# A register as scale of the exponentials, and ScalarE instead of VectorE as reader of the first feed-forward layer's sums

## The chip, the cores and the metric

The kernel runs on one core of one Trainium2 chip. A core has four engines that compute: TensorE (PE in the profile) multiplies matrices into PSUM, VectorE (DVE), ScalarE (ACT) and GpSimd (POOL) do the elementwise work; SyncE (SP) issues the transfers. Each engine works through a queue of its own in order, and engines wait for each other on semaphores. The metric is the device time of one execution in microseconds (us), as the median of several runs. A profile, taken in a run of its own, shows when each instruction ran.

## The reference

One transformer block in which attention and a feed-forward network work in parallel on the same normalized input. All is float32, with 2048 rows of 512, 32 heads of 16, and 1792 hidden units.

```python
xn = _layernorm(x)
qkv = (xn @ wqkv) ...                       # 32 heads of 16
scores = einsum("bhqd,bhkd->bhqk", q, k) * 16 ** -0.5
p = softmax(scores); o = einsum("bhqk,bhkd->bhqd", p, v)
A = o.reshape(B, S, D) @ wo
h = gelu(xn @ w1 + b1)                      # tanh form
B = h @ w2 + b2
out = x + A + B
```

## The kernel before

**Numbers.** Float32 operands are divided by powers of two and split into a high and a low float16 part; a product is three float16 products (`PAIRS`). The factors come back later as scales: `sexp` (line 95) has, for each of four sets of eight heads, the factor of the scores times 16 ** -0.5, the same number in all 128 partitions; `fac1` has the factors of the first layer's weights, `gs` those of the others.

**The loop.** Attention is cut into 32 tiles: eight groups of four heads by four blocks of 512 queries. A tile has 16 units, one for each block of 128 keys, so there are 512 units (`NU`, line 387). `unit` (line 626) writes out one unit in two halves. In each half, TensorE computes two heads' scores in a first orientation (`s_half`, line 238, into a bank called pS), and VectorE takes their maximum (line 250). It also computes, for a unit that lies 19 (`LEAD`) back, two heads' scores in the transposed orientation with the maximum already subtracted (`e_half`, line 284, into pT), and ScalarE takes their exponential (line 295) into a buffer pe. Then it multiplies the exponentials of a still earlier unit with the values (`v_half`, line 298, into pV), and beside that, on the other 64 rows of the array, it does a few products of the dense work (`dense`, line 568, into pD). So in each unit VectorE has four reductions, ScalarE four exponentials, and TensorE's order of work is fixed by the order in which the program is written.

**Banks.** PSUM has eight banks: three for pS, three for pT, one for pD and one for pV at the start (`free_banks`, line 102). A dense group takes a bank when it begins (`dbank`, line 398) and gives it to the pT banks when it ends, so that the next group takes its bank from these: pD and pT share four banks, of which pD holds one. `tiled` and `product` (lines 195 and 167) issue all these products, so most of TensorE's rows carry line 169.

**The dense work.** Three generators feed the groups (`Group`, line 404): `rest` (the projections to queries and keys, whose sums ScalarE reads at line 495), `mlp` (line 995) and `tail` (the output projection, read at line 1100 while attention runs and at line 1093 after its scores are done). `mlp` runs four times over 512 rows: 14 groups of the first layer, 12 products for each side, at a pace of 4 or 3 products a half unit (`FAST`, `SLOW`), then four groups of the second layer with 42 products a side. When a first-layer group is over, `hidden` (line 1033) reads its sums out of PSUM, multiplies by the factor, adds the bias and writes hh (line 1036, VectorE). One unit later `gelu` (line 1001) begins: three steps on GpSimd, a tanh on ScalarE (line 1005), four more on GpSimd. When a second-layer group is over, ScalarE reads its sums (line 1059, yt). At the end of each tile ScalarE reads pV (line 321, osb).

**Bookkeeping.** `later` and `pooled` place work by slots, one slot a unit. `given` (line 159) adds an estimated time to `backlog`, which each half unit lowers by 1300 ns (line 660); no other line reads it.

Of the kernel before, what the change touches and what calls it, by code (L numbers as in the profile page):

```python
# [10 lines left out]
I32 = mybir.dt.int32  # L11
AF = mybir.ActivationFunctionType
ALU = mybir.AluOpType
# [14 lines left out]
NQB = S // QB  # L28
# [19 lines left out]
def layer_kernel(ctx: ExitStack, tc: tile.TileContext, x, wqkv, wo, w1, b1, w2, b2, out):  # L48
    nc = tc.nc
# [45 lines left out]
    sexp = const.tile([P, 4], F32, name="sexp")  # L95
# [11 lines left out]
    def banks(tag):  # L107
        k = free_banks[tag].pop(0)
        free_banks[tag].append(k)
        return bank_tile(k, tag)  # L110
# [48 lines left out]
    def given(engine, ns):  # L159
        backlog[engine] += ns  # L160
# [26 lines left out]
    def enter():  # L187

        if left:
            goal[0] = f"turn{counted[0]}"  # L190
            for p in left:
                tc.add_to_no_dep_group(goal[0], p.ins)
            left.clear()

    def tiled(user, dst, lhs, rhs, start, stop):

        for j in range(0, P, 32):
            product(user, dst[j:j + 32], lhs[:, j:j + 32], rhs, start=start, stop=stop)


    mt_of, ptiles, pv_of, stores = {}, {}, {}, {}
    queue, slot = [], [0]

# [22 lines left out]
    def tick():  # L226
        run_due()
        run_steps()
        slot[0] += 1
# [54 lines left out]
    def e_half(u, n):  # L284

        p, a = divmod(n, 2)
        t, kt = divmod(u, 16)
        g, qb = divmod(t, NQB)
        st = banks("T")
        r = slice(64 * a, 64 * a + 64)  # L290
        k0 = (kt % 4) * P
        tiled(None, st, kst[g % 2][p][kt // 4][r, k0:k0 + P], qst[g % 2][p][qb][r, :], True, True)
        pe = work.tile([P, QB], F32, name="pe", bufs=12)
        ptiles[u, n] = pe
        nc.scalar.activation(pe, st, AF.Exp, scale=sexp[:, g // 2:g // 2 + 1])  # L295
        given("act", 580)

    def v_half(u, a):

# [87 lines left out]
    NU = NG * NQB * 16  # L387
# [171 lines left out]
    def burst(gen, n):  # L559

        while n > 0 and (f := group(gen)) is not None:
            if not f.usable():
                break
            f.product(2)
            n -= 1
            ended()
# [59 lines left out]
    def unit(gen):  # L626


        u = pos[0]
        e = u - LEAD  # L630
        if u == LEAD and cur[0] is not None:
            burst(gen, cur[0].left())
        pos[0] += 1
        for a in range(2):
            for b in range(2 * a, 2 * a + 2):
                if u < NU:
                    s_half(u, b)
                elif u > NU:
                    spare(gen, b % 2)
                if 0 <= e < NU:  # L640
                    e_half(e, b ^ 1)
            if u < LEAD:
                burst(gen, LFILL[u - 16] // 2)
            if e >= 0:
                enter()

                w, r = (e - 2, 1) if a == 0 else (e - 1, 0)
                live = 0 <= w < NU
                new = r == 0 and w % 16 == 0
                if live and not new:  # L650
                    v_half(w, r)
                dense(gen, 1 - r)
                if live and new:
                    v_half(w, r)

                for user, goes_on in (("V", live and not (r == 1 and w % 16 == 15)),
                                      ("D", cur[0] is not None and not cur[0].over())):
                    leave(user, goes_on)
                for k in backlog:
                    backlog[k] = max(0, backlog[k] - HALF)  # L660
                if live and r == 1:
                    v_end(w)
                ended()

            if a == 0 and u % 16 == 0 and u // 16 - 1 in stores:
                stores.pop(u // 16 - 1)()
        if u < NU:
            s_end(u)
        tick()
# [325 lines left out]
    def mlp():  # L995
        m2 = st2p
        w2_s = m2.tile([P, 2, NF, D], F16, name="w2_s")
        b2_b = m2.tile([P, D], F32, name="b2_b")
        done = set()

        def gelu(hh, g, b, f):
            t1 = m2.tile([P, QB], F32, name="t1", bufs=2)

            def tanh():
                nc.scalar.activation(t1, t1, AF.Tanh, scale=GELU_C * GELU_A)
                given("act", 600)
                later(1, rest, True)

            def rest():
                pooled((690, lambda: nc.gpsimd.tensor_scalar(t1, t1, 1.0, gs[:, 1:2], op0=ALU.add, op1=ALU.mult)),  # L1010
                       (1280, lambda: nc.gpsimd.tensor_tensor(t1, t1, hh, op=ALU.mult)),  # L1011
                       (620, lambda: nc.gpsimd.tensor_scalar(g[:, 0, f, :], t1, 1.0, 0.0, op0=ALU.mult, op1=ALU.add)),
                       (1160, lambda: nc.gpsimd.tensor_tensor(g[:, 1, f, :], t1, g[:, 0, f, :], op=ALU.subtract)),  # L1013
                       (0, lambda: done.add((b, f))))

            pooled((1040, lambda: nc.gpsimd.tensor_tensor(t1, hh, hh, op=ALU.mult)),  # L1016
                   (620, lambda: nc.gpsimd.tensor_scalar(t1, t1, 1.0, 1.0 / GELU_A, op0=ALU.mult, op1=ALU.add)),
                   (1280, lambda: nc.gpsimd.tensor_tensor(t1, t1, hh, op=ALU.mult)),  # L1018
                   (0, lambda: later(2, tanh, True)))

        for b in range(NQB):
            xb = xbs[b]
            g = m2.tile([P, 2, NF, QB], F16, name="g", bufs=1)
            for f in range(NF):
                later(1, lambda n=b * NF + f + 2: fetch_w1(n))
                wc = wcs[b * NF + f]
                if b == 0 and f >= 3:
                    for k in range(f - 3, NF if f == NF - 1 else f - 2):
                        later(2 * (k - f + 3), lambda k=k: nc.sync.dma_start(w2_s[:, :, k], w2_d[:, :, k]))
                if b == 0 and f == 3:  # L1030
                    nc.sync.dma_start(b2_b, b2[None, :].to_broadcast([P, D]))

                def hidden(hp, g=g, b=b, f=f):
                    hh = m2.tile([P, QB], F32, name="hh", bufs=3)
                    scale, bias = fac1[0][:, f // 2:f // 2 + 1], b1_s[:, f:f + 1]
                    nc.vector.tensor_scalar(hh, hp, scale, bias, op0=ALU.mult, op1=ALU.add)  # L1036
                    given("dve", 700)
                    later(1, lambda: gelu(hh, g, b, f), True)

                yield Group([lambda c=c, i=i, j=j, wc=wc, xb=xb: (wc[:, i, c, :], xb[:, j, c, :])  # L1040
                             for c in range(NC) for i, j in PAIRS], dbank, hidden, pace=FAST if f % 2 else SLOW)
            for q in range(4):
                t = b * 4 + q
                xa = m2.tile([P, D], F32, name="xa", bufs=2)
                if q == 1:
                    fetch_x(b + 1)
                if b == NQB - 1 and q == 1:

                    ocs[2] = feed[0].tile([P, 2, NC, QB], F16, name="xb", bufs=1)
                    when((NG - 2) * NQB + 2, lambda: read_o(ocs[2], 2, True), 2)  # L1050
                    for k in range(3):
                        acs[8 + k] = feed[0].tile([P, D], F32, name="ac", tag="wc", bufs=3)
                        later(3 + k, lambda k=k: read_acc(acs[8 + k], 8 + k))
                nc.sync.dma_start(xa, x[t * P:(t + 1) * P, :])
                later(3, lambda xa=xa: pooled((1280, lambda: nc.gpsimd.tensor_tensor(xa, xa, b2_b, op=ALU.add))), True)

                def store(yp, xa=xa, t=t):
                    yt = m2.tile([P, D], F32, name="yt", bufs=2)
                    nc.scalar.activation(yt, yp, AF.Copy, scale=gs[:, 2:3])  # L1059
                    given("act", 600)  # L1060
                    add = lambda: nc.gpsimd.tensor_tensor(xa, xa, yt, op=ALU.add)  # L1061
                    put = lambda: nc.sync.dma_start(acc_d[t * P:(t + 1) * P, :], xa)
                    later(1, lambda: pooled((1280, add), (0, lambda: later(4, put, True))), True)

                yield Group([lambda f=f, i=i, j=j, q=q, g=g: (g[:, i, f, q * P:(q + 1) * P], w2_s[:, j, f, :])
                             for f in range(NF) for i, j in PAIRS], dbank, store,
                            lambda n, b=b: (b, n // 3) in done, pace=SLOW if b < 2 else MEAN)
# [151 lines left out]
```

## Time and profile before

| | |
|---|---|
| median of 3 runs | 1535.31 us (1532.46 to 1536.68) |
| span of the profiled execution | 1533.9 us |
| TensorE's mean granted clock | 0.995 of full speed |
| exponentials, line 295 | 2048, from 120.3 to 1516.5 us |
| first-layer reads, line 1036 | 56, from 318.8 to 1270.1 us |
| second-layer reads, line 1059 | 16, from 480.2 to 1397.4 us |

A row of a group gives line, engine, operation, what is written and read with shapes, the count, and after the bar the busy time in us, the mean duration of one in ns, and the idle time of the engine just before them with what ended it. Instructions of one engine overlap at their ends, so the busy time of many is less than count times mean. A timeline row gives start, length and the number of merged instructions. A row of the chain of waits gives start, length and the work that the end waited for at that time. The stretches of the windows view give the stretch, its length, an engine's busy time with its instructions, the granted clock, and the transfers.

### The profile page before, as it was taken

How to read it: one execution, taken by the hardware profiler on the slowest of the kernel's cores; microseconds unless marked ns; L12 is line 12 of the kernel's file. 1: busy time of each engine (PE TensorE's matmuls, PEld its weight loads, DVE VectorE, ACT ScalarE, POOL GpSimd, SP SyncE). 2: the span in 40 equal slices, each digit the busy share in tenths (PEclk: the TensorE clock that was granted, in tenths of full speed). 3: DMA queues.
4: the chain of work that ended last, by engine and by line, in shares of the span. 5: the costliest groups of instructions: out<-in, count | busy, mean ns of one | idle time of the engine just before them, and what ended most of it. 6: DMA issues, size and time to landing. Idle time of an engine off the chain costs nothing. (4 is left out here: it accounts for less than half of the span.)

```text
span 1533.9 us, 86854 instructions
## 1 busy us (share of the span) xinstructions
PE 1499.4 (98%) x39407; PEld 820.3 (53%) x39407; DVE 1430.3 (93%) x2423; ACT 1374.1 (90%) x2262; POOL 662.8 (43%) x686
## 2 busy tenths in 40 slices
PE   8999999999999999999999999999999999999998
PEld 4434555555555555555555555555555555555553
DVE  7899988999999999999999999999999999999933
ACT  4318988999999999999999999999999999999995
POOL 4114597547771112777311167751117775111110
PEclk9999999999999999999999999999999999999998
DMA  6454567542122211131111211122102201111412
GB/s 205 129 154 153 168 214 214 172 124 77 56 70 66 60 29 39 37 82 50 29 42 46 60 42 39 36 77 63 35 25 59 71 25 29 49 60 55 133 58 96
DMA packets 113674, 123.76 MB, mean 81 GB/s; under 512 B 24988, under 2 KB 85276, under 8 KB 113304
## 3 DMA queue, kind: packets, MB, share of 16 engines
q1 hardware_dynamic: 113304, 118.21, 25.8%
q8 instruction: 308, 5.05, 1.4%
q14 instruction: 62, 0.51, 0.1%
HBM read 80.61 MB, written 37.34 MB: 77 GB/s over the span
## 5 line engine op out<-in xcount | busy, mean ns | idle before, releaser
L250 DVE TENSOR_REDUCE mt<-pS 128x1 f32<-128x512 f32 x2048 | 1293.2, 682 | 36.0 <-PE pS L169 18.5
L295 ACT ACTIVATE pe<-pT,sexp 128x512 f32<-128x512 f32 x2048 | 1268.5, 688 | 63.8 <-PE pS L169 21.0
L169 PE MATMUL pV<-pe,vv 64*32 64x512 f32 x8192 | 1077.0, 595 | 0.5 <-issue 0.5
L169 PE MATMUL pT<-qst,kst 64*32 64x512 f16 x8192 | 719.7, 378 | 4.1 <-issue 2.2
L169 PE MATMUL pS<-kst,qst 62*32 62x512 f16 x8192 | 624.8, 378 | 16.7 <-DVE mt L250 12.9
L169 PEld LDWEIGHTS <-qst 62*32 62x32 f16 x8192 | 279.8, 92 | 240.0 <-issue 97.0
L169 PEld LDWEIGHTS <-kst 64*32 64x32 f16 x8192 | 298.2, 91 | 174.2 <-issue 73.1
L169 PE MATMUL pD<-w_s,g 64*32 64x512 f16 x5376 | 365.1, 377 | 0.0
L169 PE MATMUL pD<-xb,wc 64*32 64x512 f16 x5376 | 360.6, 377 | 0.0
L169 PEld LDWEIGHTS pV<-pe,vv 64*32 64x32 f32 x8192 | 181.8, 105 | 84.1 <-PE pV L169 4.3
L1061 POOL TENSOR_TENSOR xa<-xa,yt 128x512 f32<-128x512 f32 x16 | 20.4, 1277 | 314.9 <-ACT yt L1059 314.9
L169 PEld LDWEIGHTS <-wc 64*32 64x32 f16 x5376 | 120.5, 91 | 53.2 <-issue 2.1
L169 PEld LDWEIGHTS <-g 64*32 64x32 f16 x5376 | 111.9, 91 | 47.0 <-issue 0.7
L169 PE MATMUL pD<-xt,wqk_h 64*32 64x512 f16 x2016 | 133.7, 378 | 0.8 <-issue 0.7
L1016 POOL TENSOR_TENSOR t<-hh 128x512 f32<-128x512 f32 x56 | 58.2, 1039 | 138.8 <-DVE hh L1036 127.5
L351 POOL TENSOR_TENSOR osb<-osb,rb 128x512 f32<-128x512 f32 x31 | 39.8, 1284 | 143.6 <-DMA rb<-den_d 77.8
L1018 POOL TENSOR_TENSOR t<-t,hh 128x512 f32<-128x512 f32 x56 | 71.7, 1281 | 4.7
L1011 POOL TENSOR_TENSOR t<-t,hh 128x512 f32<-128x512 f32 x56 | 71.6, 1278 | 4.7
L1013 POOL TENSOR_TENSOR g<-t,g 128x512 f16<-128x512 f32 x56 | 65.2, 1164 | 4.7
L169 PEld LDWEIGHTS <-wqk_h 64*32 64x32 f16 x2016 | 46.6, 92 | 21.0 <-issue 4.1
L169 PE MATMUL pD<-wo_s,oc 64*32 64x512 f16 x828 | 54.4, 378 | 0.0
L1036 DVE TENSOR_SCALAR hh<-pD,fac,b_s 128x512 f32<-128x512 f32 x56 | 45.3, 809 | 2.3 <-PE pT L169 0.8
(141 smaller groups left out, 859.1 us busy)
## 6 DMA issues: line engine op xcount, KB each, us to landing
wch<-in_B_w_dram SPq DMA_DIRECT2D x28, 512.0 KB
wc<-w_d SPq DMA_DIRECT2D x56, 256.0 KB
qk_d<-stg SPq DMA_DIRECT2D x32, 256.0 KB
rb<-den_d SPq DMA_DIRECT2D x124, 64.0 KB
w_d<-wsp SPq DMA_DIRECT2D x28, 256.0 KB
kst<-qk_d SPq DMA_DIRECT2D x128, 48.0 KB
qst<-qk_d SPq DMA_DIRECT2D x128, 48.0 KB
xs<-in_A_x_dram SPq DMA_DIRECT2D x16, 256.0 KB
```

Of the source, the lines that this page charges most:

```text
L169: p = nc.tensor.matmul(*args, **kw)
L250: nc.vector.reduce_max(mt_of[t][:, n, qt, kb:kb + 1], s, axis=AX.X)
L295: nc.scalar.activation(pe, st, AF.Exp, scale=sexp[:, g // 2:g // 2 + 1])
L351: pooled((1280, lambda: nc.gpsimd.tensor_tensor(osb, osb, rb, op=ALU.mult)), (620, lambda: nc.gpsimd.tensor_scalar(ot[:, 0], osb, 1.0, 0.0 ...
L1011: (1280, lambda: nc.gpsimd.tensor_tensor(t1, t1, hh, op=ALU.mult)),
L1013: (1160, lambda: nc.gpsimd.tensor_tensor(g[:, 1, f, :], t1, g[:, 0, f, :], op=ALU.subtract)),
L1016: pooled((1040, lambda: nc.gpsimd.tensor_tensor(t1, hh, hh, op=ALU.mult)), (620, lambda: nc.gpsimd.tensor_scalar(t1, t1, 1.0, 1.0 / GELU_A ...
L1018: (1280, lambda: nc.gpsimd.tensor_tensor(t1, t1, hh, op=ALU.mult)),
L1036: nc.vector.tensor_scalar(hh, hp, scale, bias, op0=ALU.mult, op1=ALU.add)
L1061: add = lambda: nc.gpsimd.tensor_tensor(xa, xa, yt, op=ALU.add)
```

## The change

The exponentials' scale is no longer read from `sexp` in SBUF by each instruction. `fetch_scale` allocates a register of ScalarE and loads one number of `sexp` into it, at the start of units 0, 128, 256 and 384 of the exponentials; `e_half` passes the register. `hidden` runs on ScalarE, as an Identity activation with the factor as scale and the bias as bias, both still read from SBUF. The two estimates given to the bookkeeping change with it.

```diff
+    scale_of = {}
+
+    def fetch_scale(m):
+
+        scale_of[m] = nc.scalar.alloc_register(f"sexp{m}")
+        nc.scalar.reg_load(scale_of[m], sexp[0:1, m:m + 1].bitcast(I32))
+
...
         pe = work.tile([P, QB], F32, name="pe", bufs=12)
         ptiles[u, n] = pe
-        nc.scalar.activation(pe, st, AF.Exp, scale=sexp[:, g // 2:g // 2 + 1])
-        given("act", 580)
+        nc.scalar.activation(pe, st, AF.Exp, scale=scale_of[g // 2])
+        given("act", 520)
...
         u = pos[0]
         e = u - LEAD
+        if e >= 0 and e % (2 * NQB * 16) == 0 and e < NU:
+            fetch_scale(e // (2 * NQB * 16))
         if u == LEAD and cur[0] is not None:
             burst(gen, cur[0].left())
...
                     scale, bias = fac1[0][:, f // 2:f // 2 + 1], b1_s[:, f:f + 1]
-                    nc.vector.tensor_scalar(hh, hp, scale, bias, op0=ALU.mult, op1=ALU.add)
-                    given("dve", 700)
+                    nc.scalar.activation(hh, hp, AF.Identity, scale=scale, bias=bias)
+                    given("act", 700)
                     later(1, lambda: gelu(hh, g, b, f), True)
```

## The prediction

> **What bounds the kernel now.** I read the page's busy times first, then cut the span into stretches and asked each for the exponentials alone (line 295), because there are four in every unit of the attention loop, so their rate is the rate of the loop.
>
> ```profile
> span 1533.9 us, 86854 instructions
> PE 1499.4 (98%) x39407; PEld 820.3 (53%) x39407; DVE 1430.3 (93%) x2423; ACT 1374.1 (90%) x2262; POOL 662.8 (43%) x686
> ```
> ```profile
> 317.00:445.00 128.00, 115.17 (x186) 1.00 0.28 81
> 447.00:597.00 150.00, 141.67 (x232) 1.00 0.17 47
> 598.00:727.00 129.00, 115.95 (x188) 1.00 0.20 57
> 729.00:880.00 151.00, 142.00 (x232) 1.00 0.16 45
> 880.00:1009.00 129.00, 116.10 (x187) 1.00 0.15 43
> ...
> 1143.00:1272.00 129.00, 115.87 (x187) 1.00 0.18 51
> ```
>
> Three engines are nearly full, so shares alone decide nothing. The second fence (stretch, length, ScalarE's busy time and instructions on line 295) does. The stretches 317, 598, 880 and 1143 are those in which the first feed-forward layer runs beside attention; 447 and 729 hold the second layer. First-layer stretches: 128 + 129 + 129 + 129 = 515 us for 186 + 188 + 187 + 187 = 748 exponentials, 0.6885 us each. Second-layer stretches: 301 us for 464, 0.6487 us each. The attention work per exponential is the same in both. So the first layer costs (0.6885 - 0.6487) x 748 = 29.8 us over the pace that the same loop keeps elsewhere. With 14 groups to a stretch that is 29.8 / 56 = 0.53 us for each `hidden`.
>
> What differs is VectorE. Next: durations by group of instructions, then the timeline around one `hidden` of the fourth first-layer stretch.
>
> ```profile
> L250 DVE TENSOR_REDUCE mt<-pS 128x1 f32<-128x512 f32 x2048 | 1293.2, 682 | 36.0 <-PE pS L169 18.5
> L295 ACT ACTIVATE pe<-pT,sexp 128x512 f32<-128x512 f32 x2048 | 1268.5, 688 | 63.8 <-PE pS L169 21.0
> ...
> L1036 DVE TENSOR_SCALAR hh<-pD,fac,b_s 128x512 f32<-128x512 f32 x56 | 45.3, 809 | 2.3 <-PE pT L169 0.8
> ```
> ```profile
> 1231.08 0.81 DVE L1036 TENSOR_SCALAR hh<-pD,fac,b_s 128x512 f32<-128x512 f32 x1
> 1231.81 4.86 DVE L250 TENSOR_REDUCE mt<-pS 128x1 f32<-128x512 f32 x8
> ```
>
> Instructions overlap, so what counts is the pitch from start to start. Eight queued reductions take 4.86 us: (4.86 - 0.68) / 7 = 0.597 us. `hidden` holds the queue for 1231.81 - 1231.08 = 0.73 us. A first-layer group lasts three units (pace 4,4) or four (3,3), 3.5 on average, that is 14 reductions and one `hidden`: 14 x 0.597 + 0.73 = 9.09 us of VectorE, before the small work at each tile's end. TensorE's pace of the second-layer stretches is 14 x 0.6487 = 9.08 us for the same. So in these stretches VectorE is the bound, with nothing left to catch up with. The chain of waits in that window shows how it reaches TensorE:
>
> ```profile
> 1231.10 0.79 DVE hh L1036
> 1231.89 0.61 DVE mt L250
> 1232.50 0.04 issue
> 1232.54 0.40 PE pS L169 x4
> ```
>
> The reduction behind `hidden` is late, it frees its score bank late, and TensorE, which issues in order, waits to write the next scores.
>
> **The exponential's scale.** Scale comes from SBUF now, one value per partition. The trace has no activation with a register as scale; it has some with a constant.
>
> ```profile
> L321 ACT ACTIVATE osb<-pV 128x512 f32<-128x512 f32 x32 | 19.1, 598 | 3.2 <-issue 3.2
> L495 ACT ACTIVATE pf<-pD 128x512 f32<-128x512 f32 x22 | 13.2, 599 | 5.4 <-PE pD L428 2.9 <-PE pT L169 1.5 <-PE pS L169 1.0
> L1059 ACT ACTIVATE yt<-pD,gs 128x512 f32<-128x512 f32 x16 | 11.1, 693 | 0.0
> ```
> ```profile
> 62.38 0.59 ACT L771 ACTIVATE xt<-pD 128x512 f16<-128x512 f32 x1
> 62.86 0.60 ACT L774 ACTIVATE pf<-pD 128x512 f32<-128x512 f32 x1
> ```
> ```profile
> 1218.97 4.81 ACT L295 ACTIVATE pe<-pT,sexp 128x512 f32<-128x512 f32 x8
> ```
>
> A copy without an SBUF operand takes 0.598 us, one with a scale from SBUF (yt) 0.693, the exponential 0.688: the operand costs 0.09 us. Queued copies start 62.86 - 62.38 = 0.48 us apart, queued exponentials (4.81 - 0.69) / 7 = 0.589. A register lies between two bounds: as a constant (pitch 0.589 - 0.09 = 0.50), or no gain at all (0.589). I take the constant's, since a register names no place in SBUF to be read per partition; the other bound is a rival below.
>
> 2048 x 0.09 = 184 us of ScalarE goes, but ScalarE sets the pace nowhere in the steady loop: even with 14 x 0.589 = 8.25 us plus one tanh per group it stays under 9.08. Its direct worth is therefore nothing; TensorE covers it. If that cover went, it would be worth up to 0.09 an exponential. Its indirect worth is room for `hidden`.
>
> Four register loads are new, one ahead of units 0, 128, 256 and 384 of the exponentials. Behind them queue the exponentials, and behind these TensorE's next score bank. No row shows one. Bounds: nothing, and the dearest load that ScalarE makes in this trace (second row; the first is for later):
>
> ```profile
> L754 ACT ACTIVATE xs<-xs,sd 128x512 f32<-128x512 f32 x6 | 4.0, 709 | 0.0
> ...
> L295 ACT ACT_TABLE_LOAD x1 | 1.3, 1283 | 0.0
> ```
>
> So 0 to 4 x 1.3 = 5.2 us; I take 2, as ScalarE's spare time hides part. The Trainium skill ("Runtime: NRT & Kernel Launch", "Instruction fetch mechanics") puts such a load at about 0.2 us a register; by that, an estimate of 0.8 us in place of 2, and no run here shows it yet.
>
> **`hidden` on ScalarE.** VectorE loses 56 x 0.73 = 41 us, all of it in the bound stretches. ScalarE gains an Identity with two SBUF operands, which no row shows. Duration: 0.598 + 2 x 0.09 = 0.78 us; pitch 0.48 + 2 x 0.09 = 0.66, bounds 0.48 and VectorE's 0.81. ScalarE per group: 14 x 0.50 + 0.53 (tanh, estimated as its 0.627 less the same 0.10 overlap) + 0.66 = 8.2 us, 0.9 below TensorE's 9.08.
>
> ```profile
> L1005 ACT ACTIVATE t<-t 128x512 f32<-128x512 f32 x56 | 35.1, 627 | 0.0
> ```
>
> So neither engine bounds the stretch and its pace becomes TensorE's, but for what is late next: the two exponentials queued behind the Identity, each holding a bank that TensorE wants. The second layer already shows this case, its sums being read by ScalarE (yt):
>
> ```profile
> 480.23 0.69 ACT L1059 ACTIVATE yt<-pD,gs 128x512 f32<-128x512 f32 x1
> 480.81 3.06 ACT L295 ACTIVATE pe<-pT,sexp 128x512 f32<-128x512 f32 x5
> ```
> ```profile
> 480.12 0.63 PE L169 MATMUL pV<-pe,vv 64*32 64x512 f32 x4
> 480.39 0.40 PE L169 MATMUL pD<-w_s,g 64*32 64x512 f16 x4
> ...
> 481.54 0.40 PE L169 MATMUL pT<-qst,kst 64*32 64x512 f16 x4
> ...
> 481.76 0.61 PE L169 MATMUL pV<-pe,vv 64*32 64x512 f32 x4
> ```
> ```profile
> 802.23 0.62 PE L169 MATMUL pV<-pe,vv 64*32 64x512 f32 x4
> ...
> 803.49 0.63 PE L169 MATMUL pV<-pe,vv 64*32 64x512 f32 x4
> ```
>
> An undisturbed half unit lasts 803.49 - 802.23 = 1.26 us, up to 1.28; the one after yt lasts 481.76 - 480.12 = 1.64. So 0.36 us is lost: first the new group's pD starts at 480.39, 0.27 after pV, waiting for an exponential's bank; then pT at 481.54 waits for the exponential that started at 480.81 behind yt. With exponentials 0.09 shorter, and two in a row, the first bank comes 0.18 earlier. For the second, the Identity starts 0.1 to 0.2 earlier, is 0.09 longer, and the exponential behind it 0.09 shorter: 0.1 to 0.2 earlier. Most of the 0.36 goes. Bounds 0 and 0.36; I take 0.15, since a tanh sometimes falls in the same place.
>
> Gain: (0.53 - 0.15) x 56 = 21 us; bounds 9.5 (0.36 stays) and 29.8.
>
> A rule speaks against the move: the Trainium skill ("ScalarE: Activation LUTs", "Rules for kernel authors") sends multiply and add to VectorE, up to about three times faster in bf16. This case's rows differ for float32 out of PSUM (0.809 on VectorE, 0.693 for yt on ScalarE); what the rule would do is a rival below.
>
> **Other edits.** The same shorter queue serves the sums that ScalarE reads already: 16 yt, 22 pf, and 8 of the last projection, 46 in all. At most 0.2 us each, 9 us; at least 0, where something else holds TensorE. I take 4. The counters fed by `given` are added up and decayed but nothing reads them, so order and transfers stay as they are. Identity seems to need no table of its own: the trace runs it at line 754 (row above) with no load of its own; GpSimd waits for hh and gets it no later.
>
> **Sum**, against the profiled execution: 1533.9 - 21 - 4 + 2 = 1510.9. The median of the runs, 1535.3, lies 1.4 us above that span: **1512 us**.
>
> **Rivals.** *More gain:* turnover costs nothing and every ScalarE-read sum gains: 29.8 + 9 = 39 us, 1497. For it: exponentials finish well before the banks' next use; against it, tanh.
>
> *The stall changes sides:* the turnover after `hidden` stays at yt's 0.36, nothing comes from the others, loads cost 5.2: 9.5 - 5.2 = 4 us, 1531. For it: yt shows just that today; against it, exponentials were longer there.
>
> *No effect:* the 0.53 is TensorE's own cost of starting a group, whoever reads: 1535 to 1537. Against it: the chain names `hidden` and the reduction.
>
> *Slower, the register saves nothing:* ScalarE per group is then 14 x 0.589 + 0.53 + 0.66 + 0.1 (osb) = 9.54 us. It bounds from 9.08 on, a pitch of 0.556. VectorE's 9.09 shows as 9.64 (14 x 0.6885), 0.55 over its sum, of which tile-end work takes a part; with 0.35 to 0.55 over 9.54 the group lasts about 10.0, 0.35 more: 56 x 0.35 + 2 = 22 us, 1557. For it: no row shows the register's cost.
>
> *Slower, ScalarE is the dear reader:* an Identity that holds ScalarE for three times `hidden`'s 0.73 gives 7.0 + 0.53 + 2.2 + 0.1 = 9.8 us; with 0.45 over it 10.25, 56 x 0.6 = 34 us more, 1569. This is the skill's rule taken at its word. Against it: yt's 0.693.
>
> **How the numbers follow.** Forecast 0.56, more gain 0.12, stall changes sides 0.13, no effect 0.05, register saves nothing 0.12, dear reader 0.02. The forecast's own range is 1500 to 1525; with the neighbouring cases 1496 to 1533, leaving out the slower ones and the tails. What a measurement of this kernel can tell from no change is about 0.3%, 4.6 us. Faster: 0.56 + 0.12 + 0.08 of the changed-sides case = 0.76; same: 0.05 of that case and 0.05 = 0.10; slower 0.14.
>
> **What the changed profile would show.** Right: exponentials near 0.60 us; Identity near 0.78; the first-layer stretches at 0.65 to 0.665 us an exponential while the second-layer ones stay near 0.649; VectorE near 1385 us busy; fewer waits of TensorE on the reductions. Wrong: exponentials still at 0.688, or first-layer stretches still at 0.68 with waits on ScalarE where those on VectorE stood, or four gaps of over 1.3 us on ScalarE at the register loads.

## The result and the profile after

| | before | changed |
|---|---|---|
| median | 1533.46 us (1530.91 to 1536.68, 8 runs) | 1522.28 us (1520.55 to 1530.02, 8 runs) |
| ratio | | 0.9939 (95% interval 0.9923 to 0.9955) |
| span of the profiled execution | 1533.9 us | 1518.8 us |

The change makes the kernel faster, by 0.6%, 9 to 11 us. The forecast was 1512 us, a gain of 23 us: right in sign, inside its range, and more than twice too large.

The page of the changed kernel: span, busy times, and the groups that answer to those shown of before (reductions, exponentials, `hidden`; the lines have moved by a few).

```profile
span 1518.8 us, 86848 instructions
...
PE 1489.5 (98%) x39407; PEld 815.9 (54%) x39407; DVE 1402.2 (92%) x2367; ACT 1245.6 (82%) x2318; POOL 664.5 (44%) x686
...
L257 DVE TENSOR_REDUCE mt<-pS 128x1 f32<-128x512 f32 x2048 | 1304.5, 684 | 52.5 <-PE pS L169 34.8
L302 ACT ACTIVATE pe<-pT 128x512 f32<-128x512 f32 x2048 | 1100.8, 599 | 162.9 <-PE pS L169 78.6
...
L1045 ACT ACTIVATE hh<-pD,b_s,fac 128x512 f32<-128x512 f32 x56 | 43.6, 779 | 9.4 <-PE pT L169 3.3
```

Each of the changed instructions costs what was forecast. The exponential fell from 0.688 to 0.599 us, so a register counts as a constant; the Identity takes 0.779. ScalarE's busy time fell by 128 us. VectorE's fell by 28 to 1402 us, not to the 1385 forecast, because the reductions' own busy time rose from 1293.2 to 1304.5 us. The four register loads were bounded at 1.3 us each; they appear as one line of the view by source line, with minimum, median and maximum in ns:

```profile
L206 ACTq TENSOR_LOAD <-sexp x4: 275/286/675, 117.8 to 1159.2; - x4
```

They lie beside running activations, and the view shows nobody that waited for them. The Trainium skill ("Runtime: NRT & Kernel Launch", "Instruction fetch mechanics") has about 0.2 us a register, for loads that it describes as coming from HBM. This kernel loads from SBUF: the trace's median of 0.28 us is near that figure, the first load's 0.68 is not.

The stretches tell where the gain is missing. The columns are stretch, length, ScalarE's busy time with its exponentials, clock and transfers; the stretches have moved with the kernel.

```profile
315.00:441.00 126.00, 97.74 (x183) 1.00 0.27 82
443.00:589.00 146.00, 122.02 (x227) 1.00 0.16 46
595.00:721.00 126.00, 97.65 (x184) 1.00 0.20 58
722.00:874.00 152.00, 126.68 (x235) 1.00 0.15 45
875.00:1000.00 125.00, 97.43 (x184) 1.00 0.14 44
...
1135.00:1260.00 125.00, 96.76 (x183) 1.00 0.18 52
```

First-layer stretches (315, 595, 875, 1135): 502 us for 734 exponentials, 0.6839 us each, against 0.6885 before and 0.65 to 0.665 forecast. Second-layer stretches (443, 722): 298 us for 462, 0.6450 each, against 0.6487. So the distance between the two, which the change was forecast to close, is (0.6839 - 0.6450) x 734 = 28.6 us, as good as the 29.8 of before. What came instead is a little everywhere. (The stretches are cut at whole microseconds, and 1 us in 128 is 0.005 us an exponential.)

The view of waits (us in total, times, longest) shows the other side of it. Before:

```profile
PE pS L169 <- DVE mt L250: 12.9, 54, 1.4
...
PE pT L169 <- ACT pe L295: 1.4, 4, 0.6
```

And after:

```profile
PE pT L169 <- ACT pe L302: 7.9, 20, 0.7
...
PE pS L169 <- DVE mt L257: 3.6, 14, 1.4
```

TensorE waits for VectorE's reductions less and for ScalarE's exponentials more. With the first-layer pace still at 0.68, this is the second of the signs by which the prediction said that it would be wrong. Most of a stall does not appear in these totals, since TensorE's modelled ends cover it; the half units show it whole. ScalarE's timeline around one `hidden` of the changed kernel:

```profile
1192.93 0.78 ACT L1045 ACTIVATE hh<-pD,b_s,fac 128x512 f32<-128x512 f32 x1
1193.61 0.62 ACT L1014 ACTIVATE t<-t 128x512 f32<-128x512 f32 x1
1194.13 2.05 ACT L302 ACTIVATE pe<-pT 128x512 f32<-128x512 f32 x4
```

TensorE's timeline there, pV rows alone (a half unit runs from its first pV to the next half unit's first):

```profile
1192.76 0.63 PE L169 MATMUL pV<-pe,vv 64*32 64x512 f32 x4
1193.21 0.61 PE L169 MATMUL pV<-pe,vv 64*32 64x512 f32 x4
1194.98 0.61 PE L169 MATMUL pV<-pe,vv 64*32 64x512 f32 x4
```

And the chain of waits of the same window:

```profile
1193.61 0.62 ACT t L1014
1194.22 0.50 ACT pe L302
1194.72 0.04 issue
1194.76 0.40 PE pT L169 x4
```

The half unit lasts 1194.98 - 1192.76 = 2.22 us instead of 1.28. The tanh of an earlier group stands right behind the Identity, because `hidden` is issued at the end of a unit's second half and tanh at the unit's end. So no exponential starts between 1192.93 and 1194.13, 1.2 us; the first one behind holds the bank that the half unit's second pT wants, and that pT starts 0.04 us after it ends.

All 56 half units after a `hidden`, each measured from its pV starts in the trace, against 1.278 us (the slower groups are those at a pace of 3 products a half unit, the faster those at 4):

| | count | lost in each |
|---|---|---|
| before, VectorE reads | 56 | 0.60 us (0.67 after the slower groups, 0.54 after the faster) |
| changed, tanh right behind the Identity | 18 | 0.93 us |
| changed, slower groups, an exponential behind it | 10 | 0.40 us |
| changed, faster groups, an exponential behind it | 28 | 0.29 us |

18 x 0.93 + 10 x 0.40 + 28 x 0.29 = 28.9 us, against 33.7 before. The stall changed engines and kept most of its size. The half unit ahead of a slower group's `hidden` lasts 1.14 us, before and after the change, so about 0.14 of each figure for the slower groups is time moved from one half unit into the next.

### The profile page after: what moved, and what is told of

The parts are those of the page before. It is cut to its first block, busy times and chain, and to the rows that moved or that the text cites. A ratio compares the mean times of both kernels' runs of the same rounds, so it can differ in the third digit from the quotient of the medians.

```text
span 1518.8 us, 86848 instructions
## 1 busy us (share of the span) xinstructions
PE 1489.5 (98%) x39407; PEld 815.9 (54%) x39407; DVE 1402.2 (92%) x2367; ACT 1245.6 (82%) x2318; POOL 664.5 (44%) x686
## 4 chain that ended last, share of the span: by engine, by line
PE 79%; DVE 16%; issue 2%; ACT 2%; DMA 1%; POOL 0%; SPq 0%; POOLq 0%
PE pV L169 23%; PE pD L169 19%; PE pT L169 17%; PE pS L169 16%; DVE mt L257 13%; PE pT L435 1%; PE pD L435 1%; DVE amx L709 1%; ACT pe L302 1%; ACT t L1014 1%; PE pT L528 1%; PE pV L528 0%; DMA m_d<-mhl 0%; DMA xs<-in_A_x_dram 0%; DMA wch<-in_B_w_dram 0%
## 5 line engine op out<-in xcount | busy, mean ns | idle before, releaser
L257 DVE TENSOR_REDUCE mt<-pS 128x1 f32<-128x512 f32 x2048 | 1304.5, 684 | 52.5 <-PE pS L169 34.8
L302 ACT ACTIVATE pe<-pT 128x512 f32<-128x512 f32 x2048 | 1100.8, 599 | 162.9 <-PE pS L169 78.6
L169 PEld LDWEIGHTS <-kst 64*32 64x32 f16 x8192 | 285.7, 91 | 203.9 <-issue 103.6
L169 PEld LDWEIGHTS <-qst 62*32 62x32 f16 x8192 | 273.3, 92 | 206.3 <-issue 58.2
L169 PEld LDWEIGHTS <-wc 64*32 64x32 f16 x5376 | 116.9, 91 | 41.6
L1045 ACT ACTIVATE hh<-pD,b_s,fac 128x512 f32<-128x512 f32 x56 | 43.6, 779 | 9.4 <-PE pT L169 3.3
```

The costliest lines, as they stand in the source:

```text
L169: p = nc.tensor.matmul(*args, **kw)
L257: nc.vector.reduce_max(mt_of[t][:, n, qt, kb:kb + 1], s, axis=AX.X)
L302: nc.scalar.activation(pe, st, AF.Exp, scale=scale_of[g // 2])
L1045: nc.scalar.activation(hh, hp, AF.Identity, scale=scale, bias=bias)
```

## The experiments

Each ratio is to the kernel before in the same session.

### e1 and e2: each part alone

e1 keeps `hidden` on VectorE:

```diff
-                    nc.scalar.activation(hh, hp, AF.Identity, scale=scale, bias=bias)
-                    given("act", 700)
+                    nc.vector.tensor_scalar(hh, hp, scale, bias, op0=ALU.mult, op1=ALU.add)
+                    given("dve", 700)
```

> Only the exponentials' scale comes from a register; hidden stays on VectorE as before. Theory A (the stall changed sides: hidden on ScalarE costs TensorE as much as on VectorE, and the gain came from shorter exponentials everywhere): 1522 to 1526 us, close to the changed kernel, with first-layer stretches still near 0.685 us an exponential. Theory B (the prediction's: shorter exponentials are worth nothing themselves, the gain is hidden's move into the room they leave): 1531 to 1534 us.

Measured: 1527.89 us, ratio 0.9959 (0.9945 to 0.9972). Its first-layer stretches:

```profile
316.00:443.00 127.00, 101.33 (x185) 1.00 0.29 82
597.00:726.00 129.00, 102.52 (x187) 1.00 0.21 57
878.00:1007.00 129.00, 102.70 (x188) 1.00 0.16 45
1138.00:1267.00 129.00, 102.40 (x187) 1.00 0.18 51
```

514 us for 747, 0.6881 each: the pace of before, as far as stretches of whole microseconds can tell. So shorter exponentials do next to nothing while VectorE reads the first layer's sums, and are worth about 6 us elsewhere. The time lies between the ranges of the two theories, nearer to A. The move of `hidden` then adds about 3 us (0.9959 to 0.9939), with intervals that overlap.

e2 keeps the scale in SBUF and moves `hidden`:

```diff
-        nc.scalar.activation(pe, st, AF.Exp, scale=scale_of[g // 2])
+        nc.scalar.activation(pe, st, AF.Exp, scale=sexp[:, g // 2:g // 2 + 1])
...
-            fetch_scale(e // (2 * NQB * 16))
+            pass
```

> Only hidden goes to ScalarE; the exponentials read their scale from SBUF as before. Theory A: ScalarE has 14 x 0.589 + 0.53 + 0.66 + 0.1 = 9.5 us per first-layer group against TensorE's 9.08 and hidden stands ahead of the next exponentials: slower than before, 1540 to 1557 us. Theory B (VectorE was the bound and is relieved): 1525 to 1533 us.

Measured: 1543.33 us, ratio 1.0060 (1.0045 to 1.0076). As theory A has it: without the shorter exponentials ScalarE has no room, and its half units after `hidden` lose 1.03, 0.59 and 0.38 us in the three classes above. The Trainium skill's rule to keep multiply and add on VectorE ("ScalarE: Activation LUTs", "Rules for kernel authors") comes out right here, though not for the price of the instruction, which is lower on ScalarE (0.78 against 0.81 us), but for what queues behind it.

### e3 and e12: tanh taken away from behind `hidden`

```diff
-                   (0, lambda: later(2, tanh, True)))
+                   (0, lambda: later(2, lambda: mids.append(tanh), True)))
...
+            if a == 0:
+                run_mids()
```

> The changed kernel with each tanh issued after the first half of the next unit instead of at the end of the unit, so that it never stands right behind hidden. Theory A (18 of the 56 half units after hidden lose 0.93 us because tanh follows hidden on ScalarE, the others 0.3 to 0.4): 18 x 0.6 = 10 us less, 1510 to 1514 us, and no half unit of 2.2 us after hidden. Rival C (what counts is how much work ScalarE has in the stretch, not where it stands): within 3 us of 1522.

Measured: 1515.74 us, ratio 0.9872 (0.9856 to 0.9888), 0.67% or 10 us below the changed kernel's ratio. First-layer stretches:

```profile
320.00:445.00 125.00, 98.50 (x185) 1.00 0.28 81
597.00:722.00 125.00, 98.59 (x186) 1.00 0.21 59
875.00:1000.00 125.00, 98.69 (x186) 1.00 0.16 44
1133.00:1258.00 125.00, 98.81 (x186) 1.00 0.19 52
```

500 us for 743, 0.6729 each. The half units after `hidden` lose 0.41 (slower groups) and 0.30 us (faster ones); the class of 0.93 is gone. Theory A holds in its gain and its mechanism, though the time is 2 us above its range, and rival C, that ScalarE's load alone counts, falls: the load is the same.

e12 makes the same edit on the kernel before, as a control.

> The kernel before with e3's edit alone: tanh after the first half of the next unit, hidden on VectorE, scale from SBUF. Theory A (tanh costs only where it follows hidden on the same engine): within 0.3% of before, 1530 to 1538 us. Rival M (the unit's end is a bad place for tanh whatever reads the sums): 5 us or more below before.

Measured: 1537.21 us, ratio 1.0016 (1.0005 to 1.0027). With `hidden` on VectorE moving the tanh gains nothing; if anything it costs 0.16%. What e3 gains comes from the pair, not from the tanh alone.

### e4 and e10: the sums read later

A turnover is the place where one dense group ends and the next one begins. e4 issues the read behind the next half unit's two exponentials, e10 between them; the bank returns to the list there.

```diff
+            if hold_it:
+                held.append(done)
+            else:
+                done.end()
...
+                settle()
                 ended(True)
```

> The changed kernel with the reading of a finished dense group's sums issued half a unit later, behind the next two exponentials instead of ahead of them (hidden, yt, pf and ys alike); the bank goes back to the list then. tanh stays at the unit's end and so is half a unit away from hidden. Theory A (the place ahead of the next half unit's exponentials is what costs): most of the 28 us lost after hidden and half of what is lost after yt goes, 1494 to 1505 us. Rival D (the bank comes back too late, so TensorE waits for a bank instead): 1520 us or more.

Measured: 1516.78 us, ratio 0.9880 (0.9865 to 0.9895). That is e3's gain and not more, and tanh is away from `hidden` here too; the time lies between the ranges of theory A and rival D. The half units still lose 0.38 (slower groups) and 0.22 us (faster ones), by their medians. That most of the loss would go, as theory A had it, is not so. ScalarE, then TensorE, at one turnover of e4:

```profile
655.60 1.08 ACT L303 ACTIVATE pe<-pT 128x512 f32<-128x512 f32 x2
656.57 0.78 ACT L1057 ACTIVATE hh<-pD,b_s,fac 128x512 f32<-128x512 f32 x1
```
```profile
655.29 0.63 PE L169 MATMUL pV<-pe,vv 64*32 64x512 f32 x4
655.52 0.59 PE L169 MATMUL pD<-xb,wc 64*32 64x512 f16 x5
...
656.24 0.40 PE L169 MATMUL pT<-qst,kst 64*32 64x512 f16 x4
656.73 0.40 PE L169 MATMUL pT<-qst,kst 64*32 64x512 f16 x4
```

The second pT starts at 656.73, right after the two exponentials end (655.60 + 1.08 = 656.68). No read stands ahead of them; but the old group's bank is still unread and the new group has taken another, so pT has two banks in turn instead of three and waits for an exponential a step earlier.

> The changed kernel, but a finished group's sums (hidden, yt, pf, ys) are read between the two exponentials of the next half unit, and its bank goes back to the list there, between the two pT; tanh stays at the unit's end. Theory L (what is left is ScalarE's 0.66 us standing ahead of an exponential whose bank is wanted 1.3 us later; between the two, both banks are ready in time): half units after hidden lose 0.1 to 0.2 us, about as in e9 where the read was cut, 1498 to 1506 us. Rival D (as in e4, the later return of the bank eats the gain): 1513 us or more.

Measured: 1524.84 us, ratio 0.9941 (0.9925 to 0.9957). Theory L fell. The half units lose 0.58 and 0.41 us, although tanh is away from `hidden` here too. In one of them:

```profile
655.40 0.60 ACT L303 ACTIVATE pe<-pT 128x512 f32<-128x512 f32 x1
655.89 0.77 ACT L1057 ACTIVATE hh<-pD,b_s,fac 128x512 f32<-128x512 f32 x1
```
```profile
656.05 0.40 PE L169 MATMUL pT<-qst,kst 64*32 64x512 f16 x4
656.72 0.40 PE L169 MATMUL pT<-qst,kst 64*32 64x512 f16 x4
```

Now pT waits for the bank of the sums, which the Identity frees at 655.89 + 0.77 = 656.66. That is rival D's mechanism.

### e5, e6, e7 and e11: the new group takes its bank first

```diff
+            if 0 <= e and u < NU:
+                f = group(gen)
+                if f is not None and f.bank is None:
+                    f.bank, f.key = f.alloc()
```

> The changed kernel, but a new dense group takes its bank at the start of its first half unit, ahead of the two pT of that half, so that it gets the bank that has been free longest. Theory F (at a turnover four banks serve two dense groups and pT: until the old group's sums are read, pT has two banks; taking them in another order only moves the wait from the group's start to pT): 1515 to 1522 us. Rival G (the start of the new group is what waits, 0.17 to 0.27 us each time): 46 + 56 turnovers at 0.17 or more, 1508 us or less.

Measured: 1525.19 us, ratio 0.9937 (0.9914 to 0.9961), the changed kernel's own, and 3 us above theory F's range. Rival G falls. yt's half units go from 0.25 to 0.18 us lost, and the whole does not notice.

> Both edits of e3 (tanh half a unit away from hidden) and e5 (the new group takes its bank first) on the changed kernel. Theory F (taking banks in another order moves the wait and saves little): 1511 to 1517 us, near e3. Rival G: 1505 us or less.

Measured: 1514.91 us, ratio 0.9873 (0.9856 to 0.9889), against e3's 0.9872. e6 and e3 are the fastest versions that compute the whole block, 1.3% faster than the kernel before.

> The kernel before with the same edit: hidden on VectorE, exponentials with their scale from SBUF, the new group's bank taken first. If VectorE bounds the first-layer stretches, as the prediction said, little changes there: 1528 to 1534 us. If the 0.53 us per hidden was mostly TensorE's own turnover, 56 x 0.2 and more goes: 1522 us or less.

Measured: 1536.76 us, ratio 1.0014 (0.9998 to 1.0031). The time is above both stated ranges and, within its interval, that of before. The half units after `hidden` shrink here, from 0.60 to 0.42 us lost, but those ahead of them grow as much: from 1.14 to 1.44 us at the slower groups, from 1.30 to 1.40 at the faster ones. So the edit moved the wait by half a unit and did not shorten it, and this run does not tell VectorE's bound from a cost of TensorE's own; e9 does.

> e10 with the new group's bank taken first, as in e5. Theory L: the group's start does not wait any more either (0.1 to 0.17 us at each turnover), 1493 to 1504 us, 2 to 10 us below e10. Rival F (the order of banks moves the wait only): within 2 us of e10.

Measured: 1524.70 us, ratio 0.9943 (0.9927 to 0.9958), the same as e10, as rival F had it.

### e8: no bank changes hands

```diff
-                dense(gen, 1 - r)
+                if not rests:
+                    dense(gen, 1 - r)
```

with a bank of its own for both layers (given back to the list of pD), the read between the next two exponentials, and the paces named below.

> The changed kernel with one dense bank kept for both feed-forward layers and three for pT throughout; a finished group's sums are read between the two exponentials of the next half unit, in which no dense product is issued; the pace becomes 4,4 (first layer) and 3,4 (second) so that a group with its rest lasts about as long as before. Theory F: nobody waits for a bank at a turnover, first-layer stretches run at the second layer's pace of 0.645 to 0.65 us an exponential, about 25 us less than the changed kernel: 1493 to 1502 us. Rival H (ScalarE's own load or tanh sets the first-layer pace): 1512 us or more.

Measured: 1519.85 us, ratio 0.9903 (0.9877 to 0.9928). It lies below the changed kernel, far above theory F's 1493 to 1502, and where rival H put it. The half unit that rests is 0.1 us shorter than usual, and the one after it 0.3 longer. Several things were changed at once, so this run does not tell which of them took the gain, nor whether rival H's reason is the right one.

### e9: the read cut short

```diff
-                    nc.scalar.activation(hh, hp, AF.Identity, scale=scale, bias=bias)
+                    nc.scalar.activation(hs, hp[:, 0:8], AF.Identity, scale=scale, bias=bias)
...
-                    later(1, lambda: gelu(hh, g, b, f), True)
+                    later(1, lambda: gelu(hz, g, b, f), True)
```

> e3 with hidden cut to 8 of its 512 columns and the gelu fed from a constant tile, so that the first layer's values are left out of the output; groups, banks, tanh and GpSimd's work stay. Theory J (what is left after hidden, 0.3 to 0.4 us, is ScalarE's time in the Identity, 0.66 us ahead of the next exponentials): the half units after hidden lose 0.1 us or less and the kernel takes 1496 to 1501 us. Rival K (what is left is the turnover itself: the new group's bank and TensorE's own order): they still lose 0.25 us or more, 1509 to 1516 us.

Measured: 1501.90 us, ratio 0.9785 (0.9766 to 0.9804), 1 us above theory J's range. ScalarE at one turnover of it, and its first-layer stretches:

```profile
630.81 0.36 ACT L1055 ACTIVATE hh<-pD,b_s,fac 128x8 f32<-128x8 f32 x1
631.07 1.07 ACT L308 ACTIVATE pe<-pT 128x512 f32<-128x512 f32 x2
```
```profile
319.00:441.00 122.00, 100.63 (x187) 1.00 0.30 87
592.00:714.00 122.00, 100.81 (x187) 1.00 0.22 60
866.00:988.00 122.00, 100.64 (x187) 1.00 0.16 45
1121.00:1243.00 122.00, 100.97 (x187) 1.00 0.19 53
```

The Identity holds ScalarE for 631.07 - 630.81 = 0.26 us instead of 0.68, and the stretches take 488 us for 748 exponentials, 0.6524 each, nearly the second layer's pace. The half units after `hidden` lose 0.02 us after the faster groups (0.30 in e3) and 0.23 after the slower ones (0.41). So theory J holds for the larger part: what e3 leaves, 0.9872 - 0.9785 or 13 us, is the time of the read. The read holds TensorE up in two ways, as one turnover of e3 shows, ScalarE first and then TensorE:

```profile
636.45 0.78 ACT L1053 ACTIVATE hh<-pD,b_s,fac 128x512 f32<-128x512 f32 x1
637.13 1.07 ACT L308 ACTIVATE pe<-pT 128x512 f32<-128x512 f32 x2
```
```profile
637.28 0.40 PE L169 MATMUL pT<-qst,kst 64*32 64x512 f16 x4
...
637.77 0.40 PE L169 MATMUL pT<-qst,kst 64*32 64x512 f16 x4
```

The first pT starts at 637.28, 0.05 us after the Identity ends (636.45 + 0.78 = 637.23): by the order of the banks in the program it takes the bank of the sums. The second starts at 637.77, after the exponential right behind the Identity (637.13 + 0.60 = 637.73). Within 0.07 us, this is so for the first pT in 49 of e3's 56 half units and for the second in 53. The short read of e9 frees the bank earlier and lets the exponentials start earlier, so e9 does not tell what each of the two is worth. Of the 0.23 after the slower groups about 0.14 comes from the half unit ahead, which lasts 1.14 us here too; of the rest this study shows no cause.

## Why the prediction was off

**What bounds the kernel: right in the main.** e1 (0.6881 us an exponential with shorter exponentials) shows that ScalarE did not set the first-layer pace, and e9 that TensorE's own cost of a turnover did not: with a short read, and that on ScalarE, the pace is 0.652, as the forecast took it. So VectorE's read cost the difference. Whether VectorE was full all the time, as the sum of 9.09 us against 9.08 has it, is not shown: a group lasted 9.64 us (14 x 0.6885), and the 56 half units after `hidden` alone lose 33.7 us, as much as the 29.8 that the stretches lose as a whole.

**The register: right, and undersized.** 0.09 us off each exponential, and loads that cost nothing where 2 us were set. "Its direct worth is therefore nothing" holds in the first-layer stretches; the rest came to 4 - 2 = 2 us in the forecast and to 6 us in e1. The gain in the changed kernel's second-layer pace, 0.6487 to 0.6450, would give 0.0037 x (2048 - 748) = 4.8 us if it held wherever the first layer does not run, which is most of the 6.

**`hidden` on ScalarE: this step failed, in "I take 0.15, since a tanh sometimes falls in the same place".** The loss after `hidden` was 28.9 / 56 = 0.52 us, above even the upper bound of 0.36. So the move that was to gain 21 us gained about 3 (the changed kernel against e1). Two things were wrong in it. First, "sometimes": the program issues tanh at the unit's end, where `hidden` has just been issued, and so in 18 of 56 cases the Identity and tanh stand together for 1.2 us. That could be counted before, from the order of the program and the starts of the tanh (line 1005) in the trace of before, where one starts within 1 us of a slower group's last product in the same 18 cases; it costs 10 us (e3, with e12 as control). Second, "most of the 0.36 goes": yt itself, the model for it, still loses 0.25 us with shorter exponentials. The sum assumed that the read starts earlier when the exponentials ahead of it are shorter. It does not:

```profile
547.80 1.09 ACT L302 ACTIVATE pe<-pT 128x512 f32<-128x512 f32 x2
549.02 0.69 ACT L1068 ACTIVATE yt<-pD,gs 128x512 f32<-128x512 f32 x1
549.61 1.56 ACT L302 ACTIVATE pe<-pT 128x512 f32<-128x512 f32 x3
```

In these rows of the changed kernel the exponentials are done at 548.89, and yt starts at 549.02, after 0.13 us in which ScalarE stands idle. It does so ahead of 15 of the 16 yt and 53 of the 56 Identities. Fourteen of the 16 yt start as long after the modelled end of their group's last product as they did before the change, within 0.01 us, so what they wait for is TensorE. From there the Identity is 0.09 us longer than yt and the exponential behind it 0.09 shorter, which comes to nothing.

The prediction also left out that the read holds a bank itself. The row that shows it lies in its own window of yt, in the kernel before:

```profile
481.00 0.40 PE L169 MATMUL pT<-qst,kst 64*32 64x512 f16 x4
```

yt ends at 480.23 + 0.69 = 480.92, and this first pT starts 0.08 us later. Behind an Identity, 0.09 us longer than yt, it starts later and not earlier. The read's length costs the other 13 us (e9).

**The sign.** By the prediction's own working the gain was to come from the move. About 6 of the 9 us came from the register, to which it gave 2, so that the time fell inside the range is in part luck.

**The rivals.** "The stall changes sides" is what happened, at a price higher than it was given (0.52 us against 0.36) and with the register's worth added, which it had set at nothing. "More gain" falls by the 0.52 us, and "No effect", TensorE's own cost of a turnover, by e9. "ScalarE is the dear reader" falls by the Identity's 0.779 us. "The register saves nothing" falls by the 0.599 us; its working, that ScalarE then has too much, is e2's.

## What to carry to other kernels

Moving work from a nearly full engine to one with room gained little here, because the work's place in the new queue was wrong: room is an average, and what stands right behind the moved instruction waits for all of it. Before such a move, list what the program issues next on that engine at each occurrence, and ask which buffer each of these instructions holds and when it is wanted again; here 18 of 56 occurrences met a tanh, and a reorder of half a unit was worth more than the move itself. Where all buffers are in turn, reading later or in another order only changed which of them was late (e4, e5, e10, e11). Against that part of the loss only a shorter read helped, and that was seen in a run which leaves the first layer's values out.

## What the runs showed of the hardware

A scale from a register costs an activation as much as a constant: 0.599 us for 128 x 512, against 0.688 from SBUF and 0.598 for a copy without an SBUF operand. Loading a register from SBUF took 0.28 us, 0.68 the first time, beside running activations. An Identity over 8 columns instead of 512, with the same two SBUF operands, took 0.359 us instead of 0.779, so about 0.35 us of it does not depend on the size, by the straight line through these two.
